# Key-map exponentials ordered behind the attention's exponential on ScalarE; a two-chunk start of the first tile; two fewer opening matmuls

## Chip, cores and metric

The kernel runs on one core of a Trainium2 chip. The metric is device microseconds of that core. The kernel before takes 459.73 us (median of 3 runs, 459.2 to 460.23).

## The reference

Two attention blocks over the same input x (2048 x 1024) are mixed by a gate. Block A is linear attention over 32 heads of width 32, block B attends to 8 keys at distances 0, 2, ..., 14. Cut to what matters:

```python
g = sigmoid((x * gate_w).sum(-1, keepdims=True))

# A
phi = lambda t: where(t > 0, t + 1, exp(t)) + 1e-6
pq, pk = phi(q), phi(k)
kv = einsum("bhsd,bhse->bhde", pk, v);  z = einsum("bhsd->bhd", pk)
o = einsum("bhqd,bhde->bhqe", pq, kv) / (einsum("bhqd,bhd->bhq", pq, z)[..., None] + 1e-6)
a = o_merged @ A_wo

# B
logits = einsum("bhsd,bhswd->bhsw", q, kg) * 32 ** -0.5      # 8 gathered keys, masked at the start
b = merge(einsum("bhsw,bhswd->bhsd", softmax(logits), vg)) @ B_wo

out = g * a + (1 - g) * b
```

Each block has its own projection `x @ wqkv` (1024 x 3072) and output weights (1024 x 1024).

## The kernel before

The large products are made by `Group`, one level of Strassen-Winograd: seven products of half size instead of eight, named `m1`, `m2`, `m6`, `m3`, `m4`, `m7`, `m5`. Each has four matmuls of 128x512 in the projections (`nk=4`) and eight in the output (`nk=8`). A group has a PSUM tile X, which `m1`, `m6`, `m5` and `m3` accumulate into one after the other, and a PSUM tile Y for `m2`, then one for `m7` and `m4`. After `m1`, `m6` and `m5`, ScalarE copies the running sum of X to SBUF (`save`, L270 to L276): `M1s`, `U2s`, `U4s`. The next product that accumulates into X can't start until that copy has read it. The results are made by `final`: VectorE adds Y to one of the copies (L246), ScalarE copies X for `m3` (L244).

`run` (L427) interleaves group g with the one before it, p. The order on TensorE is

    g.m1  g.m2  p.m3  g.m6  p.m4  g.m7  g.m5

and `m5` is the product that needs the copy `U2s`. After each product `side` (L384) is called. It takes a step of the work that lies beside the products (attention, key-value sums), and `dve_side` (L405) issues at most one entry of the `deferred` lists.

Attention B (`attn`, L693) is such side work. It has for each of two chunks: `scores` (72 small matmuls into s, then one exponential `PT` of 128x2048 on ScalarE, L707, then a mask multiplication on VectorE, L708) and `pv` (72 and 8 matmuls into o, then on ScalarE a logarithm of the partial sums `rB<-o`, L729, and on VectorE a copy `nB<-o`, L730, both reading o; then a second exponential and the products `oB`, L734 and L736). All side work shares one PSUM buffer of four banks (`side_ps`, one buffer): s and o take turns in it, so the matmuls of the second `pv` wait until o of the first has been read by both engines. `nB` waits for the logarithm, too.

The key map of block A (`phi`, L549) is a list of three entries put into `deferred` by `ka_group` (L567): (1) `eA = exp(tA)` on ScalarE (L551, 128x1024) and `tA = max(tA, 0)` in place on VectorE (L552), (2) `eA = min(eA, 1) + EPS` (L553), (3) `eA = eA + tA` (L554). It is made for two row tiles per group. The results feed the matmuls `kps` (L585) of a later group.

Every engine works through its own queue in order. The order on TensorE and SyncE is the program's (`manual_schedule`, L40); on ScalarE and VectorE a scheduler puts the instructions in order, and `tc.issue_after(x)` ties an instruction behind x there, `tc.high_priority()` puts one forward. In the stage where the key groups run together with the attention, ScalarE's queue around the second `PT` is

    tA<-X, eA (tile 0), PT, U2s, eA (tile 1), U4s, rB<-o, M1s, rB, ...

This place comes seven times, at 102, 132, 162, 191, 221, 250 and 280 us.

At the start, `warm_up` (L465, called at L862) issues 14 matmuls of 128x256 on zeros while the first loads run. `vb_plain` (L509) then makes the first four row tiles with plain products. The first two tiles of x come as rows (`xr`) and are transposed by TensorE (`transpose`, L469): 8 matmuls, whose results ScalarE and VectorE copy to `xT`, each one half. The weight W comes in chunks of 256 rows, `vb_load(k, 0)`, in the order k = 0 (ScalarE's queue), 1, 2, 3 (SyncE's queue, behind the two loads of `xr`); chunk k serves kc = 2k and 2k+1 in L520.

Of the kernel before, what the change touches and what calls it, by code (L numbers as in the profile page):

```python
# [8 lines left out]
ACT = mybir.ActivationFunctionType  # L9
# [17 lines left out]
def kernel(  # L27
# [11 lines left out]
    nc = tc.nc  # L39
# [6 lines left out]
    SCALE = float(Dh) ** -0.5  # L46
# [203 lines left out]
    class Group:  # L250
# [10 lines left out]
        def mm(self, ps, m, start):  # L261
            for kc in range(self.nk):
                lhsT, rhs = self.operands(m, kc)
                nc.tensor.matmul(ps[:], lhsT=lhsT, rhs=rhs, start=start and kc == 0,  # L264
                                 stop=kc == self.nk - 1, skip_group_check=True)
# [68 lines left out]
    def row_ops(w, pair):  # L334
        p, c = divmod(pair, 4)
        return lambda m, kc: (xop(m, kc, p, slice(c * P, c * P + P)), w.get(m, kc))
# [4 lines left out]


    queue = []
    state = {"credit": 0.0, "prev": None, "steps": 0, "now": 0, "free": 0}
    deferred = []

    def add_side(delay, gen, key, kind, front=False):
# [47 lines left out]
    def defer(products, ops, gap=1):  # L395


        deferred.append([state["now"] + products, list(ops), gap])
# [46 lines left out]
    def tile_of(pair, i):  # L445
        return (pair // 4) * 8 + (pair % 4) + 4 * i
# [18 lines left out]
    def warm_up(n):  # L465
        for _ in range(n):
            nc.tensor.matmul(gps_tile[:, 1, 0:256], lhsT=warm[:, 0:P], rhs=warm, start=True, stop=True)  # L467

    def transpose(t):  # L469
        p, j = divmod(t, 8)  # L470
        hf, c = divmod(j, 4)
        for k0, tag, copy in ((0, "X1", nc.scalar.copy), (4, "Y1", nc.vector.tensor_copy)):
            tps = ps_pj.tile([P, 512], F32, name="tps", tag=tag)
            tps = tps.bitcast(BF16)[:, 0:512].rearrange("p (k n) -> p k n", k=4)
            for k in range(4):
                nc.tensor.transpose(tps[:, k, :], xr[t][:, (k0 + k) * P:(k0 + k + 1) * P], ident[:])
            with tc.high_priority():
                last_dve[0] = copy(out=xT[p][:, k0:k0 + 4, hf, c * P:(c + 1) * P], in_=tps).ins


    def v_tiles(name):
        if name == "va":
            return [tring.tile([P, H, 32], BF16, name=name, tag="t") for _ in range(2)]
        vs = [tring.tile([P, H, 33], BF16, name=name, tag="t") for _ in range(2)]
        for v in vs:
            nc.gpsimd.memset(v[:, :, 32:33], 1.0)  # L486
        return vs
# [21 lines left out]
    def vb_plain(*pairs):  # L509


        vs = {pair: v_tiles("va") for pair in pairs}
        tiles = [(pair, i) for pair in pairs for i in range(2)]

        def ps_of(pair, i):
            return ps_pj.tile([P, 512], F32, name="K", tag="XY"[i] + str(pair % 2))

        def mm(ps, pair, i, j, kc):
            p, c = divmod(pair, 4)
            nc.tensor.matmul(ps[:], lhsT=xT[p][:, kc, i, c * P:c * P + P],  # L520
                             rhs=wvB.W[:, kc, 512 * j:512 * j + 512], start=kc == 0, stop=kc == 7,
                             skip_group_check=True)
        ps = {t: ps_of(*t) for t in tiles[:2]}
        for k in range(4):
            for t in tiles[:2]:
                if k == 0:
                    transpose(tile_of(*t))
                for kc in (2 * k, 2 * k + 1):
                    mm(ps[t], *t, 0, kc)
        for t in tiles:  # L530
            if t not in ps:
                ps[t] = ps_of(*t)
                for kc in range(8):
                    mm(ps[t], *t, 0, kc)
            gate(tile_of(*t))
            v_final(vs[t[0]], True)(t[1], 0, ps[t][:], None)
        tiles = tiles[2:] + tiles[:2]
        ps = {t: ps_of(*t) for t in tiles}
        for k in range(4):
            for t in tiles:  # L540
                for kc in (2 * k, 2 * k + 1):
                    mm(ps[t], *t, 1, kc)
                if k == 3:
                    pair, i = t
                    v_final(vs[pair], True)(i, 1, ps[t][:], None)
                    vb_store(vs[pair], pair, i)


    def phi(e, t):  # L549

        return [lambda: (nc.scalar.activation(out=e, in_=t, func=ACT.Exp),  # L551
                         nc.vector.tensor_scalar(out=t, in0=t, scalar1=0.0, scalar2=None, op0=ALU.max)),  # L552
                lambda: nc.vector.tensor_scalar(out=e, in0=e, scalar1=1.0, scalar2=EPS, op0=ALU.min, op1=ALU.add),  # L553
                lambda: nc.vector.tensor_tensor(out=e, in0=e, in1=t, op=ALU.add)]  # L554
# [4 lines left out]
    def ka_group(w, pair):  # L559
        ts = [tring.tile([P, D], BF16, name="tA", tag="t") for _ in range(2)]  # L560

        def final(i, j, ps, add):
            acc(ts[i][:, 512 * j:512 * j + 512], ps, add)

        def done(i):
            e = ering.tile([P, D], BF16, name="eA", tag="e")
            defer(1, phi(e[:], ts[i][:]))  # L567
            pks[tile_of(pair, i)] = e
        return Group(row_ops(w, pair), final, done)

# [122 lines left out]
    def attn(nn, p, kT, qT, vw):  # L693


        def scores(ch):
            s = side_ps("s")
            for j in range(NPAIR):
                for b in range(2):
                    q0, n, k0 = block(j, b)  # L700
                    for g in range(4):
                        nc.tensor.matmul(s[64 * b:64 * b + 64, g, QB * j:QB * j + n],  # L702
                                         lhsT=kT[32 * g:32 * g + 32, ch, k0:k0 + 64],
                                         rhs=qT[32 * g:32 * g + 32, ch, q0:q0 + n], start=True, stop=True)
            PT = ptp.tile([P, 4, 512], BF16, name="PT", tag="PT")
            with tc.high_priority():
                nc.scalar.activation(out=PT[:], in_=s[:], func=ACT.Exp, scale=SCALE)  # L707
            nc.vector.tensor_tensor(out=PT[:], in0=PT[:], in1=maskp[:, None, :].broadcast_to([P, 4, 512]), op=ALU.mult)  # L708
            return PT

        def pv(ch, PT):
            o = side_ps("o")
            for j in range(NPAIR):
                cols = slice(QB * j, QB * j + block(j, 0)[1])
                for g in range(4):
                    for b in range(2):
                        rows = slice(64 * b, 64 * b + 64)
                        nc.tensor.matmul(o[32 * g:32 * g + 32, 2 * b, cols], lhsT=vw[rows, j, 4 * ch + g, :],  # L718
                                         rhs=PT[rows, g, cols], start=True, stop=True)
            for g in range(4):  # L720
                for b in range(2):
                    rows = slice(64 * b, 64 * b + 64)
                    nc.tensor.matmul(o[32 * g:32 * g + 32, 2 * b + 1, :], lhsT=ones[rows, :], rhs=PT[rows, g, :],  # L723
                                     start=True, stop=True)
            nB = ofp.tile([P, 2, 512], F32, name="nB", tag="nB", bufs=1)
            rB = ofp.tile([P, 2, 512], F32, name="rB", tag="rB", bufs=1)
            oB = ofp.tile([P, 1024], BF16, name="oB", tag="oB", bufs=1)
            with tc.high_priority():
                nc.scalar.activation(out=rB[:], in_=o[:, 1:4:2, :], func=ACT.Ln)  # L729
                nc.vector.tensor_copy(out=nB[:], in_=o[:, 0:4:2, :])  # L730
            nc.scalar.activation(out=rB[:], in_=rB[:], func=ACT.Exp, scale=-1.0)
            n = 8 * QB
            num, r = (ap[:, :, 0:n].rearrange("p b (j q) -> p j b q", j=8) for ap in (nB, rB))
            nc.vector.tensor_tensor(out=oB[:, 0:2 * n].rearrange("p (j b q) -> p j b q", j=8, b=2), in0=num, in1=r,  # L734
                                    op=ALU.mult)
            nc.vector.tensor_tensor(out=oB[:, 2 * n:1024].rearrange("p (b q) -> p b q", b=2), in0=nB[:, :, n:512],  # L736
                                    in1=rB[:, :, n:512], op=ALU.mult)
            nc.sync.dma_start(out=OB_d[p][2 * nn + ch, :, :], in_=oB[:])

        yield 0, 4  # L740
        PT = [scores(0)]
        yield 1, 4
        PT.append(scores(1))
        for ch in range(2):
            yield 1, 3
            pv(ch, PT[ch])
        yield 1, 3
# [111 lines left out]
        return Group(operands, final, nk=8, scale=sc)  # L859


    warm_up(14)  # L862

    wkB, wqB, wqA = {}, {}, {}

# [140 lines left out]
```

## Time and profile before

| | |
|---|---|
| median of 3 runs | 459.73 us |
| profiled execution, its own time | 459.77 us |
| its span, first to last instruction | 458.0 us |
| TensorE busy | 442.6 us (97%) |
| VectorE busy | 283.3 us (62%) |
| ScalarE busy | 237.2 us (52%) |
| granted TensorE clock | 1.000 |

The lines of the timeline have: start us, duration us, engine, source line, operation, written<-read, size, count; in brackets the idle time of the engine just before and what ended it. DMA rows on an engine's queue carry a q (SPq, ACTq). A line of the list of waits has: who waited, for whom, us in total, times, longest us. Matmuls are pipelined, so a group of four that takes 1.03 us by its own record is followed by the next one 0.865 us after its start; start-to-start times are the ones to add up. The same holds for ScalarE and VectorE, where the next instruction starts some 0.1 us before the one ahead of it ends.

### The profile page before, as it was taken

To read this page: it belongs to the slowest core of one execution; us is meant where nothing else is said; L and a number is where in the kernel's file an instruction comes from. 1 tells how busy PE (TensorE), PEld (TensorE's weight loads), DVE (VectorE), ACT (ScalarE), POOL (GpSimd) and SP (SyncE) were. 2 spreads that over 40 slices of the span, in tenths; PEclk is the share of its full clock that TensorE was granted. 3 is DMA by queue.
4 is the path that set the end of the run, shared out by engine and by line. 5 is a ranking of instruction groups with operands and counts; after the bars stand their busy time and mean duration, and the time that the engine had idled before them with its cause. 6 is when DMAs were issued, how large, how long until landed. Compare 5 with 4: busy or idle time off the path is not lost.

```text
span 458.0 us, 11713 instructions
## 1 busy us (share of the span) xinstructions
PE 442.6 (97%) x5017; PEld 216.6 (47%) x5070; DVE 283.3 (62%) x452; ACT 237.2 (52%) x345; POOL 60.1 (13%) x119
## 2 busy tenths in 40 slices
PE   8999999998999999999999999999999999999996
PEld 5454444444444444444444444445554444444444
DVE  0566668679657486484774846669777982256112
ACT  3233457467476474673846838536676544222221
POOL 8100000000000000000000000008686314000000
PEclk9999999999999999999999999999999999999999
DMA  8899801880302603007030076291229772795111
GB/s 213 194 203 269 277 2 72 239 158 26 76 4 61 132 3 99 1 27 165 5 99 3 24 156 192 77 253 47 71 79 217 164 173 92 155 204 135 48 46 47
DMA packets 111956, 51.62 MB, mean 113 GB/s; under 512 B 75552, under 2 KB 107552, under 8 KB 111904
## 3 DMA queue, kind: packets, MB, share of 16 engines
q1 hardware_dynamic: 111600, 50.61, 45.9%
q8 instruction: 39, 0.64, 0.6%
q10 hardware_dynamic: 272, 0.26, 0.2%
q14 instruction: 13, 0.11, 0.1%
q0 software_dynamic: 32, 0.00, 0.0%
HBM read 26.22 MB, written 16.78 MB: 94 GB/s over the span
## 4 chain that ended last, share of the span: by engine, by line
PE 90%; ACT 7%; issue 1%; DVE 0%; ACTq 0%; DVEq 0%
PE X L264 41%; PE Y L264 28%; PE Q L667 9%; PE K L520 3%; ACT PT L707 3%; PE o L718 2%; PE oA L624 2%; ACT eA L551 2%; PE s L702 1%; PE kps L585 1%; ACT tA L244 1%; PE o L723 1%; PE Y L299 1%; ACT U2s L273 1%; PE gps L467 1%
## 5 line engine op out<-in xcount | busy, mean ns | idle before, releaser
L264 PEld LDWEIGHTS <-xT 128*128 128x128 bf16 (+1 forms) x352 | 33.0, 98 | 39.6 <-issue 1.8
L264 PE MATMUL X<-T,SS 128*128 128x512 f16 x176 | 45.3, 380 | 0.7 <-ACT U2s L273 0.7
L264 PEld LDWEIGHTS <-WS 128*128 128x128 bf16 (+1 forms) x288 | 28.1, 98 | 33.6
L667 PE MATMUL Q<-xT,WS 128*128 128x512 bf16 x186 | 43.1, 379 | 0.3
L264 PE MATMUL X<-SS,TS 128*128 128x512 f16 x144 | 37.0, 379 | 4.0 <-ACT U2s L273 3.9
L273 ACT COPY U4s<-X 128x512 f32<-128x512 f32 x40 | 23.4, 585 | 33.2 <-PE X L264 33.1
L486 POOL MEMSET vA<- 128x32 bf16 x16 | 4.0, 250 | 268.0 <-DVE eA L554 144.8
L264 PE MATMUL Y<-W,xT 128*128 128x512 bf16 (+1 forms) x152 | 39.0, 379 | 0.0
L264 PEld LDWEIGHTS <-SS 128*128 128x128 f16 x264 | 24.3, 98 | 29.7 <-issue 2.8
L707 ACT ACTIVATE PT<-s 128x2048 bf16<-128x2048 f32 x16 | 29.9, 1870 | 15.1 <-PE s L702 15.0
L264 PE MATMUL Y<-xT,WS 128*128 128x512 bf16 (+1 forms) x144 | 37.0, 379 | 0.0
L264 PEld LDWEIGHTS <-TS 128*128 128x128 f16 x216 | 20.5, 98 | 29.0 <-issue 5.9
L708 DVE TENSOR_TENSOR PT<-PT,maskp 128x2048 bf16<-128x2048 bf16 x16 | 19.6, 1224 | 22.1 <-ACT PT L707 22.1
L273 ACT COPY M1s<-X 128x512 f32<-128x512 f32 x40 | 23.6, 591 | 11.5 <-PE X L264 10.4
L667 PEld LDWEIGHTS <-WS 128*128 128x128 bf16 x192 | 18.3, 98 | 20.1
L273 ACT COPY U2s<-X 128x512 f32<-128x512 f32 x40 | 23.4, 584 | 8.2 <-PE X L264 8.2
L264 PEld LDWEIGHTS <-oT 128*128 128x128 bf16 (+1 forms) x176 | 17.1, 98 | 20.8 <-DMA oT<-OA_d 0.5
L635 POOL TENSOR_TENSOR obA<-ofv,rec 128x512 bf16<-128x512 f32 x22 | 25.6, 1184 | 0.9
L730 DVE COPY nB<-o 128x1024 f32<-128x1024 f32 x16 | 19.5, 1222 | 6.2 <-ACT rB L729 6.2
L729 ACT ACTIVATE rB<-o 128x1024 f32<-128x1024 f32 x16 | 16.4, 1025 | 12.4 <-DVE oB L736 8.2
L264 PE MATMUL X<-T,oS 128*128 128x512 f16 x96 | 22.7, 379 | 0.0
L264 PE MATMUL X<-W,SS 128*128 128x512 bf16 x86 | 22.5, 379 | 0.1
(140 smaller groups left out, 760.1 us busy)
## 6 DMA issues: line engine op xcount, KB each, us to landing
V_d<-va SPq DMA_DIRECT2D x16, 256.0 KB, 3.2
WS<-in_B_wqkv_dram SPq DMA_DIRECT2D x16, 256.0 KB, 4.2
W<-in_A_wqkv_dram SPq DMA_DIRECT2D x8, 512.0 KB, 5.9
vw<-V_d SPq DMA_DIRECT2D x16, 256.0 KB, 4.4
OB_d<-oB SPq DMA_DIRECT2D x16, 256.0 KB, 2.2
OA_d<-obA SPq DMA_DIRECT2D x16, 256.0 KB, 2.3
out_dram<-osb SPq DMA_DIRECT2D x30, 128.0 KB, 1.8
oT<-OB_d SPq DMA_DIRECT2D x12, 256.0 KB, 4.0
```

What stands on the lines that cost most here:

```text
L264: nc.tensor.matmul(ps[:], lhsT=lhsT, rhs=rhs, start=start and kc == 0, stop=kc == self.nk - 1, skip_group_check=True)
L273: nc.scalar.copy(out=s[:], in_=ps[:])
L520: nc.tensor.matmul(ps[:], lhsT=xT[p][:, kc, i, c * P:c * P + P], rhs=wvB.W[:, kc, 512 * j:512 * j + 512], start=kc == 0, stop=kc == 7, ski ...
L551: return [lambda: (nc.scalar.activation(out=e, in_=t, func=ACT.Exp), nc.vector.tensor_scalar(out=t, in0=t, scalar1=0.0, scalar2=None, op0= ...
L624: nc.tensor.matmul(o[:, k, 132 * j:132 * j + 132], lhsT=es[i][:, j, k * P:(k + 1) * P], rhs=KVz[:, nn + 4 * j, :], start=True, stop=True)
L635: nc.gpsimd.tensor_tensor(out=ob[:, k:k + 2], in0=of[:, k:k + 2, :, 0:32], in1=rec[:, k:k + 2].broadcast_to([P, 2, 8, 32]), op=ALU.mult)
L667: nc.tensor.matmul(ps[:], lhsT=w.W[:, kc, j * P:j * P + P], rhs=xT[p][:, kc, i, :], start=kc == 0, stop=kc == 7, skip_group_check=True)
L707: nc.scalar.activation(out=PT[:], in_=s[:], func=ACT.Exp, scale=SCALE)
L708: nc.vector.tensor_tensor(out=PT[:], in0=PT[:], in1=maskp[:, None, :].broadcast_to([P, 4, 512]), op=ALU.mult)
L718: nc.tensor.matmul(o[32 * g:32 * g + 32, 2 * b, cols], lhsT=vw[rows, j, 4 * ch + g, :], rhs=PT[rows, g, cols], start=True, stop=True)
L729: nc.scalar.activation(out=rB[:], in_=o[:, 1:4:2, :], func=ACT.Ln)
L730: nc.vector.tensor_copy(out=nB[:], in_=o[:, 0:4:2, :])
```

## The change

```diff
@@
-    state = {"credit": 0.0, "prev": None, "steps": 0, "now": 0, "free": 0}
+    state = {"credit": 0.0, "prev": None, "steps": 0, "now": 0, "free": 0, "PT": None}
@@ vb_plain
-        for k in range(4):
-            for t in tiles[:2]:
-                if k == 0:
-                    transpose(tile_of(*t))
-                for kc in (2 * k, 2 * k + 1):
-                    mm(ps[t], *t, 0, kc)
+        for t, k in ((0, 0), (0, 1), (1, 0), (1, 1), (0, 2), (1, 2), (0, 3), (1, 3)):
+            if k == t == 0:
+                transpose(tile_of(*tiles[0]))
+            for kc in (2 * k, 2 * k + 1):
+                mm(ps[tiles[t]], *tiles[t], 0, kc)
+            if k == t == 0:
+                transpose(tile_of(*tiles[1]))
@@ phi
-        return [lambda: (nc.scalar.activation(out=e, in_=t, func=ACT.Exp),
+        def exp():
+            with tc.issue_after(state["PT"]) if state["PT"] else nullcontext():
+                nc.scalar.activation(out=e, in_=t, func=ACT.Exp)
+        return [lambda: (exp(),
@@ ka_group
-            defer(1, phi(e[:], ts[i][:]))
+            defer(2, phi(e[:], ts[i][:]))
@@ attn, scores
             with tc.high_priority():
-                nc.scalar.activation(out=PT[:], in_=s[:], func=ACT.Exp, scale=SCALE)
+                state["PT"] = nc.scalar.activation(out=PT[:], in_=s[:], func=ACT.Exp, scale=SCALE).ins
@@
-    warm_up(14)
+    warm_up(12)
```

The key map's exponential is tied behind the last attention exponential that was traced, and the key map is deferred by two products instead of one. In the first tile pair the two matmuls of chunk 1 for tile 0 go between the transposes of tile 1 and the matmuls that need them; the order of the others changes to match. Two opening matmuls go.

No instruction but these two matmuls goes or comes, and GpSimd's and SyncE's queues are the same. In the built program ScalarE's queue at the seven places is

    tA<-X, PT, U2s, eA (tile 0), eA (tile 1), U4s, rB<-o, M1s, rB, ...

VectorE's queue changes there, too, since L552 to L554 follow the exponentials. At 132, 191, 250 and 280 us it was, after the addition that makes kT (at 280 us vA) from M1s,

    L552 tile 0, L553 tile 0, tA<-Y,U2s, L708 mask, L554 tile 0, L552 tile 1, kT<-Y,U4s, L553 tile 1, L554 tile 1, nB, vA<-Y,M1s, oB, oB, nB

and it is now

    tA<-Y,U2s, L708 mask, L552, L553, L554 tile 0, kT<-Y,U4s, L552, L553 tile 1, nB, vA<-Y,M1s, oB, oB, L554 tile 1, nB

At 162 and 221 us, where the sums of the next weights (L131 to L134) lie at this place, it was

    L552 tile 0, L553 tile 0, tA<-Y,U2s, L708 mask, L131, L132, kT<-Y,U4s, L133, L134, nB, vA<-Y,M1s, oB, oB, L554 tile 0, L552, L553 tile 1, nB

and it is now

    tA<-Y,U2s, L708 mask, L552 tile 0, L131, L132, kT<-Y,U4s, L133, L134, nB, vA<-Y,M1s, oB, oB, L553 tile 0, L552 tile 1, L554 tile 0, nB

At 102 us, where two sets of sums meet, L552 of tile 0 goes from ahead of tA<-Y,U2s to behind the first oB pair; between them stand L133, tA<-Y,U2s, the mask, L131, L132, kT<-Y,U4s, L134, L133, nB as before. At the first key group, at 90 us, there is no attention exponential in between: ScalarE's order stays, and on VectorE tA<-Y,U2s goes one place ahead of L553.

## Prediction

> **What bounds the kernel now.** I read the page's busy times first, then the chain of waits, TensorE's list of waits, and the timeline at one of the places that the list points to.
>
> ```profile
> PE 442.6 (97%) x5017; PEld 216.6 (47%) x5070; DVE 283.3 (62%) x452; ACT 237.2 (52%) x345; POOL 60.1 (13%) x119
> ```
>
> TensorE is the engine to free: what shortens its idle time moves the end. The chain leaves TensorE at seven places, always alike; here is the fourth:
>
> ```profile
> 189.69 0.88 PE X L264 x4
> 191.27 1.06 ACT eA L551
> 192.33 1.77 ACT PT L707
> 194.62 1.02 PE X L264 x4
> ```
>
> ```profile
> PE X L264 <- ACT U2s L273: 4.6, 7, 0.7
> PE K L520 <- ACT xT L478: 0.7, 2, 0.5
> ```
>
> So m5 waits seven times for U2s, which stands behind the key exponential and PT on ScalarE. The same place in the timeline:
>
> ```profile
> 190.49 0.77 PE L702 MATMUL s<-qT,kT 32*64 32x57 bf16 x72
> 191.27 1.06 ACT L551 ACTIVATE eA<-tA 128x1024 bf16<-128x1024 bf16 x1
> 192.23 1.86 ACT L707 ACTIVATE PT<-s 128x2048 bf16<-128x2048 f32 x1
> 192.93 1.03 PE L264 MATMUL Y<-xT,WS 128*128 128x512 f16 x4
> 193.12 0.69 DVE L246 TENSOR_TENSOR tA<-Y,U2s 128x512 bf16<-128x512 f32 x1
> 193.99 0.58 ACT L273 COPY U2s<-X 128x512 f32<-128x512 f32 x1
> 194.12 1.23 DVE L708 TENSOR_TENSOR PT<-PT,maskp 128x2048 bf16<-128x2048 bf16 x1 [0.31 <-ACT PT L707]
> 194.62 1.02 PE L264 MATMUL X<-SS,TS 128*128 128x512 f16 x4 [0.67 <-ACT U2s L273]
> 195.68 0.59 ACT L273 COPY U4s<-X 128x512 f32<-128x512 f32 x1 [0.15 <-PE X L264]
> 196.61 1.02 ACT L729 ACTIVATE rB<-o 128x1024 f32<-128x1024 f32 x1 [0.34 <-PE o L723]
> 197.97 1.22 DVE L730 COPY nB<-o 128x1024 f32<-128x1024 f32 x1
> 198.24 1.03 PE L264 MATMUL X<-SS,WS 128*128 128x512 f16 x4
> 199.24 0.74 PE L718 MATMUL o<-PT,vw 64*32 64x57 bf16 x72
> ```
>
> m7 starts at 192.93, so m5 could start 0.865 later, at 193.80; it starts at 194.62. Loss: 0.82. A second limit stands just behind: p.m3 starts at 198.24 and is through at 199.10, but the second pv starts at 199.24, when nB (197.97+1.22 = 199.19) has read o. What m5 gains is kept only as far as nB also moves forward.
>
> The start:
>
> ```profile
> 4.17 1.06 PE L476 MATMUL tps<-ident,xr 128*128 128x128 bf16 x8
> 5.48 0.60 PE L520 MATMUL K<-W,xT 128*128 128x512 bf16 x2 [0.25 <-ACT xT L478]
> 5.92 0.61 PE L476 MATMUL tps<-ident,xr 128*128 128x128 bf16 x8
> 6.98 3.19 PE L520 MATMUL K<-W,xT 128*128 128x512 bf16 x14 [0.46 <-ACT xT L478]
> ```
>
> **What the Trainium skill says.** "TensorE: Matmul & The Clock Gate", its opening table, has ScalarE and VectorE as strict FIFOs: a copy can't overtake. The trace agrees: m6 is done at about 192.1, and U2s starts at 193.99 behind eA and PT. "ScalarE: Activation LUTs", section What ACT_TABLE_LOAD costs, gives 186 ns + 0.833 ns per element and an overlap of about 93 ns back to back; the trace has 1057 and 1878 ns, and starts 0.96 and 1.76 us apart, which I use. "PSUM — Partial Sum Buffer", Terms, says that ScalarE and VectorE may not read a bank of one quadrant together; the program's nB waits for the logarithm, and at 202.15 it starts 0.03 after the logarithm ends (201.10+1.02). "TensorE: Matmul & The Clock Gate", What's actually happening, has half clock until about 3.4 us of sustained work in a free-running window. In the trace 128-column transposes start 0.105 apart up to 5.0 us, but 0.055 apart at 5.92, so the clock rises between.
>
> **Part 1, the exponentials, at 191 us.** ScalarE: the scores end at 190.49+0.77 = 191.26, and PT follows 0.07 later (the gap at the first PT of a pair, 157.67 against 156.83+0.77): 191.33 instead of 192.23. U2s 1.76 later, 193.09 to 193.67. m5 needs it at 193.80: the stall goes, with 0.1 to spare. Queued behind U2s are now both eA (193.56 and 194.52; tile 1 needs tA<-Y,U2s, done at 193.81), then U4s at 195.49 to 196.07. m5 ends about 194.8, so U4s waits some 0.6 for the exponentials. Its users are p.m3, due at 197.42 (198.24 less 0.82), and kT<-Y,U4s on VectorE. The logarithm follows at 195.96 and ends by 196.98.
>
> VectorE decides nB. tA<-Y,U2s is tied to Y of p.m4, before the stall, so it stays at 193.12. The mask can follow 0.60 later (190.12 to 190.72 is that step): 193.72, since PT ends at 193.2; before it waited for PT until 194.12. To nB the steps were 3.85 (197.97-194.12). Now, with start-to-start steps from this timeline: mask 1.15, L552 0.34, L553 0.45, L554 0.60, kT 0.61, L552 0.34, L553 0.33 = 3.82. kT is reached at 196.26, after U4s (196.07), so it doesn't wait. nB: 193.72+3.82 = 197.54 instead of 197.97, also after the logarithm. Gain 0.43; the second pv starts at 198.81 instead of 199.24, and TensorE, there at 198.28, waits 0.5 where it lost 0.82. Of the stall, half moves.
>
> The same sum elsewhere, with each place's own starts:
>
> - 132 us: 135.30 becomes 134.36+0.60 = 134.96; nB 138.78 for 139.14, gain 0.36.
> - 250 us: nB 256.37 for 256.79, gain 0.42. 280 us: 285.79 for 286.28, gain 0.49.
> - 162 us: mask 164.33; L552 165.48, L131 165.82, L132 166.27, kT 166.70 (U4s ready at 166.68), L133 167.32, L134 167.66, nB 168.09 for 168.27. It ends at 169.31 and TensorE is there at 168.90 (169.72-0.82); pv starts at 169.37 for 169.80: gain 0.43. 221 us alike: 0.44.
> - 102 us: VectorE has no gap from kT to nB, and L552 leaves that stretch: its step, 0.34 (103.71 to 104.04), is the gain.
>
> Sum: 0.36+0.42+0.49+0.43+0.43+0.44+0.34 = 2.91 us.
>
> L554 of tile 1 now comes later, by up to 3 us, but lies in VectorE's wait for the second logarithm (1.17 us idle ahead of nB at 202.15) at four places; its reader kps is some 10 us later (180.34 for the map of 162 us), and a memset of vA that waits for it feeds an addition at 205.11. At 162 and 221 us the second nB stays near 172.4 (172.48 before), and U2s behind the second logarithm is done at 172.74, where m5 asks at 172.92. The deferral by two products, and the order at 90 us, touch no wait of TensorE: nothing, hidden behind its matmuls. If these covers failed, each would cost the 0.2 to 0.4 of its margin seven times at most.
>
> **Part 2, the start.** The first xr is issued at 0.74 and lands 3.2 later, at 3.94. The 14th warm-up starts at 3.95 and holds the first transpose until 4.17; with 12 the last starts at 3.53, and transposes start at about 3.97. Then: t0's pair at 5.28, t1's transposes at 5.72 to 6.16 (their xr lands at 1.21+4.1 = 5.31). The two moved matmuls need chunk 1: 1.66+4.8 = 6.46, so 6.49 to 6.92. t1's copy, 0.2 earlier than 6.93, is ready by then. Four matmuls at 0.216 bring it to 7.78, but chunk 2 lands at 2.13+5.9 = 8.03: a new wait. 8.06 plus eight matmuls is 9.79; before, 6.98+14x0.216 = 10.0. Gain 0.2, bound by the loads, not the 0.43+0.2 that the order alone would give. Bounds: 0 to 0.6, were the loads later or earlier; below nothing only through the clock, below.
>
> **Sum.** 459.77-2.91-0.2 = 456.66. The profiled run stands 0.04 above the median of 459.73, so I take 456.7, 0.66% faster.
>
> **Rivals.**
>
> *The stall moves whole to nB* (0.09): the mask or kT<-Y,U4s slips, for instance U4s behind two exponentials is 0.4 later than I sum, so nB stays. For it: at 162 us kT has 0.02 to spare; against: at the four other places 0.2. Then only the start remains: 459.6, within 0.2% (0.92 us), which is about what a measurement can tell from no change.
>
> *All stalls go* (0.06): nB doesn't bind. Seven times about 0.8, 5.6, with 0.4 to 0.6 at the start: 453.7. Against it, pv at 199.24 follows nB by 0.05 already.
>
> *The clock rises late* (0.07), the slower side: two warm-ups fewer, with TensorE idle from 3.74 to 3.97, and the gate stays at half. A 512-column matmul then costs 0.216 more. One window of 3.4 us costs half of it, 1.7, and leaves the kernel faster; from two windows on, 3.4, the gain of 3.1 is eaten. Two and a half, with some waits of Part 1 uncovered: 460.8. For it, the skill's window; against it, transposes fill the time up to 5.0 as before.
>
> *The order does nothing*: excluded at ScalarE by the queue as built; I leave 0.02, at 459.7.
>
> **How the numbers follow.** My case has 0.76: 456.7, own range 455.8 to 457.8 (0.15 on each of seven places, 0.3 at the start, 0.4 of scatter as in the three runs shown). To hold 8 in 10 with nB moving less or one late window of the clock, the range goes 455.5 to 458.7. Faster by over 0.2%: my case, all stalls go, and 0.01 of a partial slip, 0.83; same: 0.10; slower: 0.07.
>
> **What would show it.** Right: TensorE's wait of X for U2s gone; waits of o (L718) for nB of about 0.5 in their place; mask 0.6 behind tA<-Y,U2s; U4s 0.6 behind m5's end; K matmuls waiting near 8 us for W. Wrong: m5 still waiting; nB waiting behind U4s; 128-column transposes still 0.105 apart at 5.7.

## The result, and the profile after

The changed kernel takes 456.95 us (median of 4 runs, 456.67 to 458.04), the kernel before 459.59 us beside it (4 runs, 459.2 to 460.23). The ratio is 0.9946, 95% interval 0.9926 to 0.9966: 0.54% faster; the medians differ by 2.6 us. The profiled execution is the slowest of the four, 458.04 us with a span of 456.3. Its start is late, as told below.

Busy times on the page, of the changed kernel:

```profile
PE 446.7 (98%) x5068; PEld 217.3 (48%) x5068; DVE 281.2 (62%) x452; ACT 235.2 (52%) x345; POOL 60.7 (13%) x119
```

TensorE's busy time isn't larger by work: the profile has 5068 matmul records against 5017 before, though the kernel issues two fewer, so some records were missing in the earlier one (its weight loads, PEld, count 5070). The list of waits of TensorE tells more (who waited, for whom, us in total, times, longest):

```profile
PE o L722 <- DVE nB L734: 2.9, 7, 1.0
PE gps L467 <- DVE KVacc L170: 1.2, 1, 1.2
PE o L722 <- issue: 0.9, 1, 0.9
```

The seven waits of X for U2s, 4.6 us, are gone. Seven waits of o for nB, 2.9 us, stand in their place; the kernel before had one:

```profile
PE o L718 <- DVE nB L730: 0.6, 1, 0.6
```

The list shows less than the start times do (m5's loss of 0.82 at 191 us stands in it as a wait of 0.67), so the gain is read from start times below. Here is the fourth place after the change, in the timeline (L706 is L702 of before, L711 is L707, L722 is L718, L733 and L734 are L729 and L730; the exponential eA, L551 before, is L554 now, and L552 to L554 of before are L556 to L558):

```profile
190.51 0.77 PE L706 MATMUL s<-qT,kT 32*64 32x57 bf16 x72
191.35 1.88 ACT L711 ACTIVATE PT<-s 128x2048 bf16<-128x2048 f32 x1
192.95 1.03 PE L264 MATMUL Y<-xT,WS 128*128 128x512 f16 x4
193.12 0.58 ACT L273 COPY U2s<-X 128x512 f32<-128x512 f32 x1
193.15 0.69 DVE L246 TENSOR_TENSOR tA<-Y,U2s 128x512 bf16<-128x512 f32 x1 [1.72 <-PE Y L264]
193.59 2.02 ACT L554 ACTIVATE eA<-tA 128x1024 bf16<-128x1024 bf16 x2
193.76 1.21 DVE L712 TENSOR_TENSOR PT<-PT,maskp 128x2048 bf16<-128x2048 bf16 x1
193.81 1.03 PE L264 MATMUL X<-SS,TS 128*128 128x512 f16 x4
195.49 0.59 ACT L273 COPY U4s<-X 128x512 f32<-128x512 f32 x1
197.44 1.03 PE L264 MATMUL X<-SS,WS 128*128 128x512 f16 x4
197.56 1.22 DVE L734 COPY nB<-o 128x1024 f32<-128x1024 f32 x1
198.83 0.74 PE L722 MATMUL o<-PT,vw 64*32 64x57 bf16 x72 [0.36 <-DVE nB L734]
```

By chance the place starts within 0.02 us of where it did before, so the two timelines can be laid over each other. m5 now follows m7 by 0.86 (192.95 to 193.81), without a wait. p.m3 starts at 197.44 instead of 198.24, 0.80 earlier; the second pv starts at 198.83 instead of 199.24, 0.41 earlier. The difference is the wait for nB.

From the start of the second scores to the start of the second pv, at the seven places:

| place (us, before) | before | after | gained | forecast |
|---|---|---|---|---|
| 102 | 9.30 | 8.97 | 0.33 | 0.34 |
| 132 | 8.69 | 8.31 | 0.38 | 0.36 |
| 162 | 8.71 | 8.15 | 0.56 | 0.43 |
| 191 | 8.75 | 8.32 | 0.43 | 0.43 |
| 221 | 8.71 | 8.14 | 0.57 | 0.44 |
| 250 | 8.75 | 8.32 | 0.43 | 0.42 |
| 280 | 8.82 | 8.31 | 0.51 | 0.49 |
| sum | | | 3.21 | 2.91 |

Of these 3.2 us the profiled execution gave 1.3 back at the start. Its start, TensorE alone:

```profile
4.39 1.03 PE L476 MATMUL tps<-ident,xr 128*128 128x128 bf16 x8 [0.45 <-POOL maskp L217]
5.68 1.04 PE L520 MATMUL K<-W,xT 128*128 128x512 bf16 x2 [0.25 <-ACT xT L478]
6.51 1.06 PE L476 MATMUL tps<-ident,xr 128*128 128x128 bf16 x8
11.32 0.54 PE L456 MATMUL gps<-gw,xT 128*128 128x1 bf16 x16
```

Two K matmuls take 1.04 us by their records where they took 0.60 before, and the second eight transposes 1.06 where they took 0.61: TensorE is still at half its clock at 7 us. Of the 14 K matmuls that follow, the first five, from 7.36, are 0.43 us apart and the last nine 0.216, so full speed comes near 9.2. The page's clock line, which has 9 in every slice, doesn't show it. The first row tile of x lands 3.6 us after its issue here, at 0.74+3.6 = 4.34, and 3.2 before; this is what the transposes wait for, since maskp, which the line names, is not read by them. The gate's matmuls, the first after the tile pair, start at 11.32 instead of 10.02.

### The profile page after: what moved, and what is told of

Read it like the earlier page. It is cut to its first block, busy times and chain, and to the rows that moved or that the text cites. A ratio compares the mean times of both kernels' runs of the same rounds, so it can differ in the third digit from the quotient of the medians.

```text
span 456.3 us, 11766 instructions
## 1 busy us (share of the span) xinstructions
PE 446.7 (98%) x5068; PEld 217.3 (48%) x5068; DVE 281.2 (62%) x452; ACT 235.2 (52%) x345; POOL 60.7 (13%) x119
## 4 chain that ended last, share of the span: by engine, by line
PE 88%; DVE 8%; ACT 1%; issue 1%; POOL 0%; POOLq 0%; DVEq 0%; ACTq 0%
PE X L264 39%; PE Y L264 28%; PE Q L671 9%; PE K L520 3%; PE s L706 2%; DVE nB L734 2%; DVE PT L712 2%; PE oA L628 2%; PE o L722 1%; PE kps L589 1%; DVE kT L246 1%; DVE tA L556 1%; ACT U2s L273 1%; PE Y L299 1%; PE gps L456 1%
## 5 line engine op out<-in xcount | busy, mean ns | idle before, releaser
L711 ACT ACTIVATE PT<-s 128x2048 bf16<-128x2048 f32 x16 | 30.0, 1877 | 15.9 <-PE s L706 15.0
L733 ACT ACTIVATE rB<-o 128x1024 f32<-128x1024 f32 x16 | 16.5, 1034 | 13.1 <-DVE oB L740 10.8
L264 PE MATMUL X<-W,xT 128*128 128x512 bf16 x88 | 22.7, 380 | 0.0
```

Source lines behind the costliest of these rows:

```text
L711: state["PT"] = nc.scalar.activation(out=PT[:], in_=s[:], func=ACT.Exp, scale=SCALE).ins
```

## The experiments

The start of the gate's matmuls serves as the marker of the start below: 10.02 us in the profile before, 11.32 in the first profile after. "Before" is the kernel before, run on the same chip.

**The exponentials alone.** Against the changed kernel, the opening is put back:

```diff
-        for t, k in ((0, 0), (0, 1), (1, 0), (1, 1), (0, 2), (1, 2), (0, 3), (1, 3)):
...
+        for k in range(4):
+            for t in tiles[:2]:
...
-    warm_up(12)
+    warm_up(14)
```

> The exponentials' part alone: tie behind PT and deferral by two products, with the start as in the kernel before (14 opening matmuls, old order of the first tile). My theory: the seven places bring 2.9 us (0.34 to 0.49 each), so 459.6-2.9 = 456.7, and TensorE's waits show no X behind U2s and seven waits of o for nB, about 2.9 us in all, as in the changed kernel. Rival, that the start carries a good part of the gain: 457.5 or more. Rival, that the changed start costs time on average because the clock rises late (as in the profiled run of the changed kernel): this kernel beats the changed one, 456.0 to 456.5.

Measured: 456.94 us (5 runs), before 459.69, ratio 0.9941, interval 0.9930 to 0.9953. TensorE's waits for nB are seven, 2.8 us. Two lines of its start:

```profile
5.47 1.03 PE L520 MATMUL K<-W,xT 128*128 128x512 bf16 x2 [0.25 <-ACT xT L478]
6.30 0.83 PE L476 MATMUL tps<-ident,xr 128*128 128x128 bf16 x8
```

This part alone makes the whole gain: 0.0059x459.69 = 2.7 us, interval 2.2 to 3.2, beside the forecast 2.9. Both rivals fall. The lines show the late rise of the clock with all 14 opening matmuls and the old order: the two K matmuls take 1.03, and the marker is at 10.62.

**The start alone.** Against the kernel before, the opening alone is changed:

```diff
-        for k in range(4):
-            for t in tiles[:2]:
...
+        for t, k in ((0, 0), (0, 1), (1, 0), (1, 1), (0, 2), (1, 2), (0, 3), (1, 3)):
...
-    warm_up(14)
+    warm_up(12)
```

> The start's part alone: two-chunk order of the first tile and 12 opening matmuls, with the key exponentials as before. My theory of the prediction: 0.2 us gained, 459.4, where the clock has risen by the first K matmuls; where a run finds the clock still at half after 7 us, 1 us or more lost in that run, so the mean lies between 459.2 and 460.5 and the seven waits of X for U2s stand at 4.6 us as before. Rival, that the start carries the gain: 458.5 or less.

Measured: 459.57 us (13 runs), before 459.69, ratio 0.9996, interval 0.9987 to 1.0004: no difference is seen; it is at most 0.6 us faster or 0.2 slower, and the forecast gain of 0.2 lies inside that. The start of its profile:

```profile
3.84 1.03 PE L476 MATMUL tps<-ident,xr 128*128 128x128 bf16 x8
5.12 0.61 PE L520 MATMUL K<-W,xT 128*128 128x512 bf16 x2 [0.25 <-ACT xT L478]
6.65 1.46 PE L520 MATMUL K<-W,xT 128*128 128x512 bf16 x6 [0.48 <-DMA W<-in_B_wqkv_dram]
8.93 1.89 PE L520 MATMUL K<-W,xT 128*128 128x512 bf16 x8 [0.82 <-DMA W<-in_B_wqkv_dram]
```

The transposes start 0.33 earlier than before (4.17), the clock is up at 5.1, and all of it is lost to two waits for W, 0.48 and 0.82: chunk 1 lands at 1.66+4.9 = 6.56 and chunk 2 at 2.13+6.8 = 8.93 here. Marker: 10.65. That is 0.63 later than before, and still the execution is 0.2 shorter than the profiled one of before. Most of the difference comes back at 289 us, inside the last pv, where TensorE pauses for 0.2 us here and for 0.8 before; the list has this pause as a wait of o for "issue".

**14 opening matmuls in the changed kernel.**

```diff
-    warm_up(12)
+    warm_up(14)
```

> The changed kernel with 14 opening matmuls again: all else as changed. If two opening matmuls fewer leave the clock low for longer, this kernel is faster than the changed one by 0.5 to 1 us on average, 456.0 to 456.4, and its profile has 128-column transposes 0.055 us apart at the second tile. If the clock's rise only depends on where the start falls in a free-running window, it is the same as the changed kernel within 0.3 us, 456.7 to 457.2, and a late rise shows up in profiles of kernels with 14 as well.

Measured: 456.88 us (6 runs, 456.49 to 459.06), before 459.69, ratio 0.9948, interval 0.9931 to 0.9965: by the median the same as the changed kernel, to some 0.8 us either way. Its first K pair takes 1.03, so the clock is late here too, marker 10.16. So two more opening matmuls don't secure an early rise. (The 459.06 is the profiled execution, whose granted clock is half from 286.6 to 290.0 us, right behind a wait of o of 1.7 us; its waits for nB come to 2.8 us.)

**The second row tile later.**

```diff
-            defer(2, phi(e[:], ts[i][:]))
+            defer(2 + 4 * i, phi(e[:], ts[i][:]))
```

> The changed kernel with the second row tile's key map deferred by four more products, which puts its L552 and L553 behind nB on VectorE at the four places without weight sums (132, 191, 250, 280 us); ScalarE's queue is unchanged. My theory, that after the change VectorE's list ahead of nB decides the second pv: nB comes 0.5 us earlier there, bound now by the logarithm, the wait of o for nB disappears at these four places and 4x0.4 to 4x0.5 = 1.6 to 2.0 us are gained on the changed kernel: 455.0 to 455.3. Rival, that the logarithm or the matmuls themselves set the second pv, so that VectorE's list has slack: no gain, 456.7 to 457.1.

Measured: 455.24 us (4 runs, 454.91 to 455.72), before 459.69, ratio 0.9906, interval 0.9894 to 0.9919. TensorE's waits, and the place at 132 us in the timeline:

```profile
PE o L722 <- DVE nB L734: 1.4, 3, 1.0
```

```profile
136.49 1.04 ACT L733 ACTIVATE rB<-o 128x1024 f32<-128x1024 f32 x1
136.82 0.68 DVE L246 TENSOR_TENSOR kT<-Y,U4s 128x512 bf16<-128x512 f32 x1
137.57 1.22 DVE L734 COPY nB<-o 128x1024 f32<-128x1024 f32 x1
137.97 1.03 PE L264 MATMUL X<-SS,WS 128*128 128x512 f16 x4
138.93 0.74 PE L722 MATMUL o<-PT,vw 64*32 64x57 bf16 x72
```

nB now starts 0.04 after the logarithm (136.49+1.04 = 137.53), so the logarithm is its bound, and it ends at 138.79, just before p.m3 is through (137.97+0.865 = 138.84). The second pv doesn't wait. The four places go from 8.31, 8.32, 8.32 and 8.31 to 7.89, 7.88, 7.89 and 7.89: 1.7 us, and the times differ by 1.7. That VectorE's list ahead of nB was the bound at these four places after the change is shown.

**The deferral without the tie.**

```diff
-            with tc.issue_after(state["PT"]) if state["PT"] else nullcontext():
+            with nullcontext():
```

> The changed kernel without the tie behind PT, with the deferral by two products. In the built program ScalarE's queue is then as before at the seven places (eA, PT, U2s, eA), and only VectorE's list is shorter ahead of nB: L552 alone goes ahead of tA<-Y,U2s, and L554 of tile 1 behind the first oB pair. My theory, that the place of the exponential on ScalarE is what counts: the seven waits of X for U2s stay at 4.5 us, nB comes earlier at the four places without weight sums, but the matmuls reach the second pv only 0.1 us before it did, so 0 to 0.5 us are gained: 459.0 to 459.6. Rival, that the shorter list on VectorE made the gain: 457.0 to 457.5.

Measured: 459.31 us (12 runs), before 459.67, ratio 0.9993, interval 0.9984 to 1.0002.

```profile
PE X L264 <- ACT U2s L273: 4.5, 7, 0.7
PE o L722 <- DVE nB L734: 0.4, 1, 0.4
```

All seven waits for U2s are there. nB is earlier (at 132 us 7.12 after the second scores, 7.42 before), but the second pv gains 0.01 to 0.21 at a place, 0.5 in all: matmuls that arrive late have no use for an early nB. The tie is needed. So is the deferral: in a version with the tie and the deferral by one product as before, built and not run, ScalarE's queue at the seven places is the old one: eA is ahead of the second PT again. The last exponential recorded by then is the first PT of the pair, so the tie holds eA behind that one alone.

**The weight sums moved as well.** Against the changed kernel, the second row tile's key features are later as in the last but one, the sums of the narrow weights are recorded four products later and those of the wide ones four earlier:

```diff
-            defer(2, phi(e[:], ts[i][:]))
+            defer(2 + 4 * i, phi(e[:], ts[i][:]))
...
-    def load_col(into, src, col0, nn, pool=None, delay=8):
+    def load_col(into, src, col0, nn, pool=None, delay=12):
...
-    def load_k(nn, delay=8):
+    def load_k(nn, delay=12):
...
-    def load_q(nn, delay=8):
+    def load_q(nn, delay=12):
...
-        defer(15, wvA[0].sums(), 3)
+        defer(11, wvA[0].sums(), 3)
```

> The kernel with tile 1 deferred by four more products, and in addition the weight sums moved: those of the narrow weights deferred by 12 products instead of 8, those of block A's value weights by 11 instead of 15, so that none stands between kT<-Y,U4s and nB at any of the seven places. Theory: the waits of o for nB that were left (1.4 us, three places: 1.0 at 102 us, 0.2 each at 162 and 221 us) go, 455.2 becomes 453.9 to 454.3. Rival, that the moved sums delay other additions or that the sums are late for their own products: 455.2 or more, with new waits of TensorE for VectorE.

Measured: 454.94 us (4 runs, 454.14 to 455.37), before 459.67, ratio 0.9898, interval 0.9885 to 0.9912. No wait for nB stands in the list any more, but a new one does:

```profile
PE s L706 <- DVE qT L246: 0.7, 1, 0.7
```

```profile
96.39 1.22 DVE L132 TENSOR_TENSOR T<-W,T 128x2048 f16<-128x2048 bf16 x1
97.52 0.69 DVE L246 TENSOR_TENSOR qT<-Y,U2s 128x512 bf16<-128x512 f32 x1
98.27 0.50 PE L706 MATMUL s<-qT,kT 32*64 32x57 bf16 x40 [0.70 <-DVE qT L246]
```

The wide sum L132, moved away from nB, now stands ahead of qT, which the first scores need. Of the 1.4 us in the list 0.7 came back, and by the medians 0.3 are left on the kernel with tile 1 later, less than the intervals can tell. At the places themselves the theory holds: the waits for nB are gone, and six of the seven take 7.88. The rival's mechanism is seen, and the expected time is missed.

**Chunk 1 from ScalarE's queue.**

```diff
     vb_load(0, 0, nc.scalar)
+    vb_load(1, 0, nc.scalar)
     xr_load(0)
     xr_load(4)
-    vb_load(1, 0)
```

> The changed kernel with the load of weight chunk 1 issued from ScalarE's queue behind chunk 0, so that chunks 1, 2 and 3 are issued some 0.5 us earlier. If the moment of issue sets when a chunk lands, the matmuls of the first tile no longer wait for W, the gate's matmuls that follow them start at 9.4 to 9.6 us instead of 9.7 or later, and the median is 0.3 to 0.5 lower than the changed kernel's 456.9: 456.4 to 456.6. If the loads share a bandwidth that is already full, the rows of x land later instead, and the median stays at 456.7 to 457.1 or rises.

Measured: 456.5 us (5 runs, 456.27 to 457.0), before 459.67, ratio 0.9935, interval 0.9923 to 0.9948. The changed kernel's 0.9946 is inside that interval, so a gain in time isn't settled. The start of this one profile:

```profile
5.92 0.61 PE L476 MATMUL tps<-ident,xr 128*128 128x128 bf16 x8
6.37 3.38 PE L520 MATMUL K<-W,xT 128*128 128x512 bf16 x14
9.59 0.54 PE L456 MATMUL gps<-gw,xT 128*128 128x1 bf16 x16
```

There is no wait for W, and the marker, 9.59, is the earliest of all profiles.

**All of these parts, and the changed kernel again.** The first takes tile 1 later, the narrow weights' sums by 12 products and chunk 1 from ScalarE's queue; the second is the changed kernel unaltered.

> Tile 1 deferred by four more products, the narrow weights' sums by 12 instead of 8 (the value weights' sums stay as they were, since moving them made the scores at 97 us wait for qT), and chunk 1 issued from ScalarE's queue. Theory: each place's gain adds: 455.2 with tile 1 later, less 0.4 for the waits at 162 and 221 us, less 0.4 for the start: 454.2 to 454.7, with one wait of o for nB left (at 102 us, 1.0 us). Rival, that the parts share their gain (the matmuls wait elsewhere for the sums or for the loads): 455.0 or more.

> The changed kernel unaltered, beside the one with all parts, for a second sample of its time and of its start: 456.7 to 457.1. If its start is set by where the clock's rise and the loads fall in each execution, this profile's gate matmuls start at another moment than the 11.3 us of the first profile, and the seven waits of o for nB are the same 2.9 us.

Measured: all parts 455.34 us (4 runs), ratio 0.9898, interval 0.9883 to 0.9913; the changed kernel 457.41 (5 runs, 456.62 to 457.59), ratio 0.9940, interval 0.9927 to 0.9953; before 460.03 beside both. All parts are no faster than tile 1 later alone (0.9906) as far as these runs tell: the forecast of 454.2 to 454.7 is missed, and the rival's 455.0 or more came. The two profiles show why the parts don't add. At 162 and 221 us moving the sums brings 0.26 each (8.14 and 8.15 become 7.88 and 7.89). At 102 us it costs 0.25 (8.96 becomes 9.21): L131 to L133 are gone from the stretch between the mask and nB, but tile 0's L556 to L558 have moved up into it, and the wait for nB grows from 1.0 to 1.3. The start has the marker at 9.95 with a late clock, 0.27 later, and a new wait of oA for eq takes 0.2. The changed kernel again is above the expected 456.7 to 457.1, as is the kernel before beside it (460.03 where it was 459.6 to 459.7); by the ratio nothing has changed. Its second profile has the same 2.9 us of waits for nB, and another start:

```profile
6.69 3.18 PE L520 MATMUL K<-W,xT 128*128 128x512 bf16 x14 [0.48 <-DMA W<-in_B_wqkv_dram]
9.71 0.54 PE L456 MATMUL gps<-gw,xT 128*128 128x1 bf16 x16
```

The same program has its marker at 9.71 here and at 11.32 in its first profile, 1.6 later; the first execution took 458.04 us and this one 456.62, 1.4 less.

## Why the prediction was right, and where it was off

The forecast was 456.7 us, 3.1 gained. The measured median is 456.95, 2.6 gained with an interval of 1.6 to 3.4 (0.0034 to 0.0074 of 459.59).

*The stall goes at m5, and half of it moves to nB.* Right, in mechanism and size. At 191 us the prediction had U2s at 193.09 (193.12 measured), m5 at 193.80 (193.81), U4s at 195.49 (195.49), nB at 197.54 (197.56), the second pv at 198.81 (198.83). What carried it: m5's gain wasn't counted as the kernel's gain, but only as much of it as VectorE's list lets nB move. Without that step the seven stalls would have been worth some 5.6 us. That the place fell within 0.02 us of where it was before is luck: the first profile had lost at the start what the places ahead of it had gained.

*The sum over the places*: 2.91 forecast, 3.21 in the profiles, 2.7 in the times of this part alone. The term that was too small is that of 162 and 221 us, 0.43 and 0.44, measured 0.56 and 0.57. There nB follows tA<-Y,U2s by 4.24 (164.32 to 168.56), and the sum had 4.36: its last step, L134 to nB, was taken as the 0.43 between them before, and it is 0.34. The step of before held a wait for the logarithm, which the change moved forward as well. The profiles give more than the times, and part of that may go into the pause inside the last pv. It is 0.2, 0.5 and 0.8 us in the three profiles in which m5 still stalls, 0.7 to 1.7 in the five with the exponentials behind PT and tile 1 not moved further, and 1.0 to 1.4 in the three that also have tile 1 later. What causes the pause isn't shown.

*VectorE's L554 of tile 1 (L558 now) and the reordered rest cost nothing*: right as far as the list of waits shows; no wait of TensorE for them appears in either profile.

*U4s 0.6 late, hidden*: as forecast. m5's matmuls are issued through at 193.81+0.865 = 194.68 and drained some 0.2 later; U4s starts at 195.49, about 0.6 after that, when ScalarE is through with the second eA. p.m3, at 197.44, doesn't wait for it.

*The start, 0.2*: the mechanism was right. Where the loads land as the sum had them, in the profile of the deferral without the tie (chunk 1 after 4.8 us, chunk 2 after 5.9), the moved pair starts at 6.55 (forecast 6.49), the first matmul of chunk 2 at 8.03 (8.06), and the marker is 9.76 (9.79). The waits for W that the lists show are mostly those for chunk 1, 0.2 to 0.5 in four profiles; one for chunk 2, 0.82, is listed for the start alone. The size doesn't hold as one number: the markers of kernels with the changed start and the loads as they were are 9.68, 9.71, 9.76, 9.77, 10.65 and 11.32, those of the old start 10.02 and 10.62. Four of the six are 0.3 earlier than before; where chunk 2 lands late or the clock rises late nothing is gained. In the times the 0.2 isn't shown: the start alone gave a ratio of 0.9996 (0.9987 to 1.0004).

*The rival of the clock*: its premise happens. In the first profile full speed comes near 9.2 us, where before it came between 5.0 and 5.5, and the kernel still gains, as the price of 1.7 allowed. Whether the two matmuls that were taken out have a part in it stays open. Against it: the clock is late with 14 opening matmuls, too (full speed near 6.7 us, in two of three profiles), and the medians with 14 and 12 agree (456.88 and 456.95). For it: the two latest rises, near 7.0 and 9.2 us, are among the eight profiles with 12, and in the latest TensorE stood idle from 3.74 to 4.39, where 14 would have kept it busy to 4.17.

## What to carry to other kernels

When a copy that TensorE waits for stands behind long instructions in an in-order queue, moving them behind it is worth only as much as the next limit allows: walk on to the next buffer that TensorE needs, and sum the list of the engine that frees it. Here 4.6 us of listed waits went and those for that buffer grew from 0.6 to 2.9, and taking the second row tile's key features out of the list ahead of it gave 1.7 us more. A tie to "the last one recorded" works only if the recording order puts the wanted instruction first; look at the queue as built before counting on it.

## What was not expected of the hardware

The start of the same program moves by 1.6 us from one execution to another (9.71 and 11.32), more than the change to it brings. Two things move. TensorE reaches full speed anywhere from 4.1 us or earlier (with tile 1 later, where the first eight transposes, from 4.14, take 0.62 and not 1.06) to about 9.2 (the first profile after). The first load of x lands 3.0 to 3.6 us after its issue, chunk 2 of W 5.7 to 6.8 where SyncE issues it behind chunk 1. Far from the start, the pause inside the last pv takes 0.2 to 1.7 us from one profile to another.
